# Sigmoid attention and a token-mixing MLP on one core: nine head groups exchange their halves by DMA instead of on GpSimd, with more buffers and a new order of work

## The chip, the core and the metric

The kernel runs on one core of a Trainium2 chip. The core has a matrix engine (TensorE, PE in the profile, its weight loads PEld), a vector engine (VectorE, DVE), an activation engine (ScalarE, ACT), GpSimd (POOL), and SyncE (SP), which here only issues DMAs. Each engine works through its own instructions in order and waits for the others by semaphores. SBUF is the on-chip memory of 128 partitions, PSUM the memory that TensorE writes. The metric is the device time of one execution in microseconds (us); the median of three runs of the kernel before is 209.17 us (208.95 to 209.36).

## The reference

Two stages, in float32, with batch B = 8, 12 heads, S = 448 tokens, 64 values per head, so D = 768:

```
scores = q @ k^T / 8 - log(448)            # per batch and head: 448 x 448
attn   = 1 / (1 + exp(-scores))            # sigmoid, no row sum
x      = attn @ v, the heads side by side  # (8, 448, 768)
wq, wk = x @ w_q, x @ w_k                  # 768 -> 64
mixed  = (wq @ wk^T / 8) @ x               # 448 x 448 token mixing, then 448 x 768
out    = max(mixed, 0) @ w_out             # 768 x 768
```

The kernel computes the mixing as wq @ (wk^T @ x), so the 448 x 448 matrix is never formed.

## The kernel before, in words

The 96 heads are handled as 24 groups n of four heads (three groups per batch). The tokens of a head are dealt to 64 positions of seven, so that a group's work falls into seven score steps, 168 in all. Work is done in these kinds of step, each with a letter in the string PLAN, and the loop at the end of the function emits the steps letter by letter. The string was written out by a planner beforehand; nothing is decided while the kernel runs.

- Loads and casts have no letter. ORDER lists them (q4, k4, v3 and so on; w0 to w6 are the weights). `pump_loads` issues a load on the SP queue as soon as, by program order, one of five load buffers (pool ld) is free; `pump` then emits the cast to bf16 on GpSimd (`cast1`, L184 and L194), provided that the cast buffers, two for q and k and three for v, are free by program order. On the chip the load waits for the cast that frees its buffer.
- q and k must be turned, so that the 64 values of a head lie on partitions. Kinds q/k and a/b do it with 56 or 14 TensorE transposes and one VectorE eviction (L242, L247). Kind c/d does it on VectorE: two stream transposes (L227) in 32 by 32 blocks of 4-byte pairs. Blocks do not cross a boundary of 32 partitions, so half of the data must first change places with its neighbour 32 partitions away. `arrange` does that on GpSimd with six copies, two each on L153, L156 and L159, of 32 partitions by 448 words. Of the 24 groups, 17 are of kind c, four of kind a (the first one included) and three of kind q.
- S is one score step: four 64 by 64 matmuls (L259) into a pair of PSUM banks and one sigmoid over 128 by 896 on ScalarE (L264). There are 168.
- P is one step of attn @ v (L277); seven of them fill a pair of banks, which VectorE evicts (L286, tile xt).
- x and X transpose xt (L317, L300) with an eviction (L330, L305); W, N, U and M are the projections, the transpose of wk, wk^T @ x, and the mixing with its relu; O is a piece of the product with w_out (L440, L475), and its last piece is evicted by VectorE (O) or ScalarE (o) and stored by DMAs on SP. Lower-case m, u and o are M, U and O with the eviction on ScalarE.
- C copies a weight tile to the other half of the partitions on VectorE (L664), six times two copies.

PSUM is handed out as four pairs of banks, so at most four of these steps can hold results that wait for their eviction. VectorE takes its instructions in the emitted order: a transpose that waits for GpSimd holds every eviction that stands behind it. `qk` tiles have eight buffers, `at` tiles 16, output tiles (`o`) three.

Of the kernel before, what the change touches and what calls it, by code (L numbers as in the profile page):

```python
# [9 lines left out]
F32 = mybir.dt.float32  # L10
BF16 = mybir.dt.bfloat16
# [6 lines left out]
def kernel(  # L18
# [43 lines left out]
    p_o = pool("o", 3)  # L62
    ps_q = pool("ps_q", 1, space=bass.MemoryType.PSUM)

# [47 lines left out]
    def xt(u, j):  # L112
# [10 lines left out]


    PLAN = (
        "SSSFFFKFSFSSSqkFPSPPPSPPPqSSSXSkSPPSPPPSSPaPSSPPPSbPPSxSSPPS"
        "SWSWWXScWSWdWPPPPSPPSPSNSUSaSbSabSSMSPCPSPMPPPSPPSPPSSWWPPSW"
        "PcdPSXSWWWSSqxkSMSPPSPPPPCSPcSoXSOSSdoSNOoSCOSPPPPSPPPCSPPPP"
        "SWWSXPSWCWSPPSUScWSSOdWOScOOSMdSPPPPMSPPSPcSONxSOSMSPPdPxSCP"
        "PPSPOSOSSWWOcWSPPPdSPPPPSOSWSSWOOWSUcSoSNOSPPPxdSPPSPcPSOOSS"  # L130
        "MPPPPSPdPPSoWSMSWOWSMWSXSPPcdPPSXSPPPSUScWSMooSdMSOWOSxOSOXS"
        "xOSOPSPPPSPPPPSPPPPScdPOSPOSOOSOOSMOSOSPPcPSdPPSPPooSONSOuSx"
        "SWWWXWWWSMOOSxoSOPcSPPPNdPSPPSoOmOOSoSoMSOOSUcSPcPSPPdPSPOPo"
        "SOSOSPPPPPPmPooSxSOdOSooSMoSoxWWWWWWSPMPPSPPcPSPOdSOONSOSoOS"
        "xoSOSooSUSoSOoSoPSoSOPPPPMPPPPPxPmPmPPWWWWoWWOxxNoouOOOMMmoO"
        "oOOOoOOoOoOoOooOoOo"
    )
    PLAN = "".join(PLAN)
    KIND = ["a"] + [t for t in PLAN if t in "qac"]

    ld = {}
    SRC = dict(q=q, k=k, v=v)
# [3 lines left out]
    def arrange(n, eng):  # L146

        arranged.add(n)
        w = pq[n].rearrange("p t e i d y -> p t e (i d y)").bitcast(U32)
        z = p_one.tile([P, 2, NI * 32], U32, tag="swap", name="swap")  # L150
        for g in range(2):
            lo, hi = slice(64 * g, 64 * g + 32), slice(64 * g + 32, 64 * g + 64)
            eng.tensor_copy(out=z[lo], in_=w[hi, :, 0])  # L153
        for g in range(2):
            lo, hi = slice(64 * g, 64 * g + 32), slice(64 * g + 32, 64 * g + 64)
            eng.tensor_copy(out=w[hi, :, 0], in_=w[lo, :, 1])  # L156
        for g in range(2):
            lo = slice(64 * g, 64 * g + 32)
            eng.tensor_copy(out=w[lo, :, 1], in_=z[lo])  # L159

    def load1(n, nm, eng):
        u, j = quads[n]
        if KIND[n] == "c" and nm != "v":
            t = p_ld.tile([P, 2 * NI * HD], F32, tag="ld", name=nm + "32")
            eng.dma_start(
                out=t, in_=SRC[nm][u, 4 * j : 4 * j + 4].rearrange("h (p r) d -> (h p) (r d)", r=2 * NI),
            )
# [3 lines left out]
        eng.dma_start(  # L171
            out=t,
            in_=SRC[nm][u, 4 * j : 4 * j + 4].rearrange(
                "(g h) (p i) d -> (h p) g (i d)", g=2, i=NI
            ),
        )
        ld[nm, n] = t

    def cast1(n, nm, eng):
        if KIND[n] == "c" and nm != "v":  # L180
# [3 lines left out]
            eng.tensor_copy(  # L184
                out=f[:, "qk".index(nm)].rearrange("p e i d y -> p e y i d"),
                in_=ld.pop((nm, n)).rearrange("p (y i e d) -> p e y i d", y=2, i=NI, e=2),
            )
# [6 lines left out]
        eng.tensor_copy(  # L194
            out=t16.rearrange("p i b d -> p b i d"),
            in_=ld.pop((nm, n)).rearrange("p b (i d) -> p b i d", i=NI),
        )
        ld[nm + "16", n] = t16
# [14 lines left out]
    def transposes_whole(ps, t16, r):  # L213

        for x, i in enumerate(range(r.start, r.stop)):
            nc.tensor.transpose(
                ps[:, x * P : (x + 1) * P], t16[:, i].rearrange("p b d -> p (b d)"), ident16,
            )

    def tr(n, nm, kind):  # L220
        t = "qk".index(nm)
        t16 = ld.pop((nm + "16", n))
        if kind in "cd":
            if t == 0:
                qk[n] = p_qk.tile([P, 2, 2, NI, NP], BF16, tag="qk", name="qk")
            assert n in arranged
            nc.vector.transpose(  # L227
                out=qk[n][:, t].rearrange("p h i n -> p (h i n)").bitcast(F32),
                in_=t16[:, t].rearrange("p e i d y -> p (e i d y)").bitcast(F32),
            )  # L230
            return
        if t == 0:
            ps_qk[n] = bank2()
        fb, _, ps = ps_qk[n]
        if kind in "ab":
            transposes_whole(ps[:, t], t16, slice(0, NI))
        else:
            transposes(ps[:, :, t * S : (t + 1) * S], t16, slice(0, NI))
        if t == 1:
            qk[n] = p_qk.tile([P, 2, 2, NI, NP], BF16, tag="qk", name="qk")  # L240
            if kind in "ab":
                nc.vector.tensor_copy(  # L242
                    out=qk[n].rearrange("p t h i n -> p t i h n"),
                    in_=ps[:, :, 0 : 2 * S].rearrange("p t (i h n) -> p t i h n", i=NI, h=2),
                )
            else:
                nc.vector.tensor_copy(  # L247
                    out=qk[n].rearrange("p t h i n -> p t h (i n)"),
                    in_=ps[:, :, 0 : 2 * S].rearrange("p h (t x) -> p t h x", t=2),
                )  # L250
            release(fb)
# [3 lines left out]
    def scores(n, i):  # L255
        fb, sc, _ = bank2()
        for g in range(2):
            for h in range(2):
                nc.tensor.matmul(  # L259
                    sc[HALF[h], g, 0:S], qk[n][HALF[g], 1, h, i, :],  # L260
                    qk[n][HALF[g], 0, h].rearrange("p i n -> p (i n)"), start=True, stop=True,
                )
        at = p_at.tile([P, 2, S], BF16, tag="at", name="at")
        nc.scalar.activation(at, sc[:, :, 0:S], ACTF.Sigmoid, bias=bias_t, scale=attn_scale)  # L264
        release(fb)
        ats[n, i] = at
# [286 lines left out]
    for t in wqks:  # L553
# [1 line left out]


    ORDER = (
# [5 lines left out]
    )  # L563
    ORDER = [(t[0], int(t[1:])) for t in ORDER.split()]
    used, loaded, cast = set(), set(), set()
# [15 lines left out]
    def pump():  # L581
        while len(cast) < len(ORDER) + 2:
# [11 lines left out]
                                in_=w32["qk"].rearrange("p (c n) -> p c n", c=NC)[HALF[h], g::2],  # L594
                            )
            else:
                back = 3 if nm == "v" else 2
                if n >= back and (nm, n - back) not in used:
                    break
                if nm != "v" and KIND[n] == "c" and n >= 2 and not {("q", n - 2), ("k", n - 2)} <= used:  # L600
                    break
                cast1(n, nm, nc.gpsimd)
            cast.add((nm, n))
# [13 lines left out]
    def tr_part(nm, t16, r, e):  # L617
        fb, _, ps = bank2()
        transposes_whole(ps[:, 0], t16, r)
        COPY[e](  # L620
            out=qk[0][:, "qk".index(nm), :, r].rearrange("p h i n -> p i h n"),
            in_=ps[:, 0, 0 : (r.stop - r.start) * P].rearrange("p (i h n) -> p i h n", h=2, n=NP),
        )
        release(fb)
# [4 lines left out]
    used |= {("q", 0), ("k", 0)}  # L629
    pump()  # L630

    done = dict.fromkeys("SPqkKxWNUMOC", 0)
    ALIKE = dict(a="q", c="q", b="k", d="k", X="x")
    done["q"] = done["k"] = 1

    for t in PLAN:
# [14 lines left out]
                pump()  # L651
        elif kind in "qk":
            tr(c, kind, t)
            used.add((kind, c))
            pump()
        elif t == "K":
            tr_part("k", k016, KB, "v")
        elif kind == "x":
# [55 lines left out]
```

## Time and profile before

| | |
|---|---|
| median of three runs | 209.17 us |
| the profiled execution: its own time / its span | 210.04 us / 208.2 us |
| granted TensorE clock, mean | 0.978 |
| busy, PE / ACT / POOL / DVE | 182.3 / 171.5 / 141.6 / 130.4 us |
| sigmoid L264: count, busy, mean | 168, 156.2 us, 1014 ns |
| stream transpose L227: count, mean | 34, 628 ns |
| GpSimd copies L153, L156, L159: count, mean | 3 x 34, 559 / 557 / 555 ns |
| HBM read / written | 35.78 / 11.01 MB |

The span is the profiled part of the execution; the execution's own time is 1.8 us longer. A busy TensorE is not TensorE at its peak, since matmuls overlap and their ends are modelled. "Idle before" is the time an engine stood still just before an instruction, with the engine and line that ended it. The sigmoids are the clock of the kernel: the first begins at 6.4 us and the last at 182.5 us, and where two follow each other directly their starts lie 0.906 us apart (the median).

### The profile page before, as it was taken

To read this page: it belongs to the slowest core of one execution; us is meant where nothing else is said; L and a number is where in the kernel's file an instruction comes from. 1 tells how busy PE (TensorE), PEld (TensorE's weight loads), DVE (VectorE), ACT (ScalarE), POOL (GpSimd) and SP (SyncE) were. 2 spreads that over 40 slices of the span, in tenths; PEclk is the share of its full clock that TensorE was granted. 3 is DMA by queue.
4 is the path that set the end of the run, shared out by engine and by line. 5 is a ranking of instruction groups with operands and counts; after the bars stand their busy time and mean duration, and the time that the engine had idled before them with its cause. 6 is when DMAs were issued, how large, how long until landed. Compare 5 with 4: busy or idle time off the path is not lost.

```text
span 208.2 us, 7853 instructions
## 1 busy us (share of the span) xinstructions
PE 182.3 (88%) x3324; PEld 110.0 (53%) x3324; DVE 130.4 (63%) x194; ACT 171.5 (82%) x197; POOL 141.6 (68%) x197
## 2 busy tenths in 40 slices
PE   7777888876889896899589699899999999999990
PEld 7343444533544352344345347676886868665560
DVE  3143455756769996955489575686867687374440
ACT  4898999986898998799779849988999989984510
POOL 2565997699899999999999999999398910000000
PEclk9999999999699999999999969999999999999997
DMA  6999988986978449876588687989475562461475
GB/s 176 362 353 265 303 284 268 348 266 217 318 242 290 155 118 324 258 278 197 180 249 289 234 251 217 296 290 340 163 214 163 172 154 51 110 154 34 137 213 151
DMA packets 24563, 47.30 MB, mean 227 GB/s; under 512 B 3792, under 2 KB 17744, under 8 KB 24528
## 3 DMA queue, kind: packets, MB, share of 16 engines
q1 hardware_dynamic: 23808, 45.42, 70.2%
q10 hardware_dynamic: 720, 1.38, 1.8%
q8 instruction: 26, 0.43, 0.8%
q14 instruction: 9, 0.07, 0.1%
HBM read 35.78 MB, written 11.01 MB: 225 GB/s over the span
## 4 chain that ended last, share of the span: by engine, by line
PE 43%; POOL 26%; DMA 11%; ACT 7%; issue 6%; DVE 4%; ACTq 1%; SPq 1%; POOLq 0%; DVEq 0%
PE banks L440 13%; PE banks L277 8%; PE banks L259 7%; PE banks L475 7%; POOL qk L184 6%; ACT at L264 6%; POOL qk L159 4%; POOL swap L153 4%; POOL qk L156 4%; DMA w<-in_moe_w_out_dram 3%; POOL v L194 3%; DMA w<-in_moe_w_k_dram 3%; PE banks L341 3%; DMA q<-in_q_dram 2%; DMA k<-in_k_dram 2%
## 5 line engine op out<-in xcount | busy, mean ns | idle before, releaser
L264 ACT ACTIVATE at<-banks,bias_t 128x896 bf16<-128x896 f32 x168 | 156.2, 1014 | 18.4 <-PE banks L259 15.8
L259 PE MATMUL banks<-qk 64*64 64x448 bf16 x672 | 63.5, 365 | 11.8 <-DVE mx L383 3.3
L277 PE MATMUL banks<-at,v 64*64 64x448 bf16 x672 | 45.6, 354 | 1.0 <-POOL v L194 0.7
L259 PEld LDWEIGHTS <-qk 64*64 64x64 bf16 x672 | 23.7, 106 | 35.5 <-issue 27.4
L440 PE MATMUL banks<-wout,mx 64*64 64x384 bf16 x672 | 35.4, 324 | 0.0
L475 PE MATMUL banks<-wout,mx 128*128 128x384 bf16 (+1 forms) x174 | 33.0, 328 | 0.1
L286 DVE CAST xt<-banks 128x896 bf16<-128x896 f32 x22 | 23.8, 1082 | 9.9 <-PE banks L277 9.7
L227 DVE STREAM_TRANSPOSE qk<-qk 128x448 f32<-128x448 f32 x34 | 20.7, 628 | 13.3 <-POOL qk L159 13.3
L277 PEld LDWEIGHTS <-v 64*64 64x64 bf16 x672 | 21.4, 107 | 12.6 <-POOL v L194 3.0
L440 PEld LDWEIGHTS <-mx 64*64 64x64 bf16 x672 | 22.9, 107 | 4.5
L383 DVE TENSOR_SCALAR mx<-banks 128x1024 bf16<-128x1024 f32 (+2 forms) x22 | 22.1, 1016 | 4.5 <-PE banks L395 3.9
L194 POOL CAST v<-v 128x896 bf16<-128x896 f32 x24 | 22.2, 932 | 3.4 <-DMA v<-in_v_dram 2.7
L184 POOL CAST qk<-k 128x896 bf16<-128x896 f32 x17 | 20.4, 1198 | 4.4 <-issue 3.1
L475 PEld LDWEIGHTS <-mx 128*128 128x128 bf16 x174 | 15.6, 99 | 13.6 <-issue 5.6
L184 POOL CAST qk<-q 128x896 bf16<-128x896 f32 x17 | 20.4, 1202 | 0.8 <-DMA q<-in_q_dram 0.6
L153 POOL COPY swap<-qk 32x448 uint32<-32x448 uint32 x34 | 19.0, 559 | 2.1
L156 POOL COPY qk<-qk 32x448 uint32<-32x448 uint32 x34 | 18.9, 557 | 2.0
L159 POOL COPY qk<-swap 32x448 uint32<-32x448 uint32 x34 | 18.9, 555 | 2.0
L341 PE MATMUL banks<-xt,wqk 128*128 128x448 bf16 x48 | 14.0, 360 | 3.3 <-DVE xt L286 2.6
L449 DVE COPY o<-banks 128x768 f32<-128x768 f32 x13 | 12.4, 955 | 6.9 <-PE banks L440 6.9
L505 DVE COPY o<-banks 128x384 f32<-128x384 f32 x20 | 11.1, 554 | 8.7 <-PE banks L475 8.3
L330 DVE COPY xn<-banks 128x1024 bf16<-128x1024 bf16 (+1 forms) x15 | 9.5, 636 | 4.5 <-PE banks L317 3.7
(68 smaller groups left out, 163.9 us busy)
## 6 DMA issues: line engine op xcount, KB each, us to landing
q<-in_q_dram SPq DMA_DIRECT2D x24, 448.0 KB, 5.0
v<-in_v_dram SPq DMA_DIRECT2D x24, 448.0 KB, 5.2
k<-in_k_dram SPq DMA_DIRECT2D x23, 448.0 KB, 5.7
out_dram<-o SPq DMA_DIRECT2D x48, 192.0 KB, 4.0
w<-in_moe_w_out_dram SPq DMA_DIRECT2D x6, 384.0 KB, 5.7
out_dram<-o ACTq DMA_DIRECT2D x6, 192.0 KB, 3.2
k<-in_k_dram SPq DMA_DIRECT2D x1, 256.0 KB, 4.5
k<-in_k_dram SPq DMA_DIRECT2D x1, 192.0 KB, 3.3
```

The costliest lines, as they stand in the source:

```text
L153: eng.tensor_copy(out=z[lo], in_=w[hi, :, 0])
L156: eng.tensor_copy(out=w[hi, :, 0], in_=w[lo, :, 1])
L159: eng.tensor_copy(out=w[lo, :, 1], in_=z[lo])
L184: eng.tensor_copy(out=f[:, "qk".index(nm)].rearrange("p e i d y -> p e y i d"), in_=ld.pop((nm, n)).rearrange("p (y i e d) -> p e y i d", ...
L194: eng.tensor_copy(out=t16.rearrange("p i b d -> p b i d"), in_=ld.pop((nm, n)).rearrange("p b (i d) -> p b i d", i=NI),)
L259: nc.tensor.matmul(sc[HALF[h], g, 0:S], qk[n][HALF[g], 1, h, i, :], qk[n][HALF[g], 0, h].rearrange("p i n -> p (i n)"), start=True, stop=True,
L264: nc.scalar.activation(at, sc[:, :, 0:S], ACTF.Sigmoid, bias=bias_t, scale=attn_scale)
L277: nc.tensor.matmul(ps[HALF[g], h, 0:S], ld["v16", n][HALF[h], i, g, :], ats[n, i][HALF[h], g, :], start=(i == 0), stop=(i == NI - 1),)
L286: nc.vector.tensor_copy(out=xt(u, j)[:, :, 0:S], in_=ps[:, :, 0:S])
L383: nc.vector.tensor_scalar(dst, ps, moe_scale, 0.0, ALU.mult, ALU.max)
L440: nc.tensor.matmul(ps[HALF[x], y, 0:NB], mx[HALF[y], u, b, 64 * (i - 3 * y) : 64 * (i - 3 * y) + 64], wout16[HALF[y], slot(y, b), x * NB : ...
L475: nc.tensor.matmul(ps, mxs[w][:, 2 * S * c + m * P : 2 * S * c + (m + 1) * P], wout16[:, c, w0:w1], start=(c == 0), stop=(c == NC - 1),)
```

## The change

Of the 24 groups seven are now of kind c (GpSimd exchanges the halves, as before), nine of a new kind e/f, six of kind q and two of kind a. A group of kind e/f is not arranged by GpSimd. VectorE transposes each of the two halves twice, once into `qk` and once into a new tile `mv` (two buffers): four stream transposes instead of two. A new step g then issues four DMAs on SP (`move`), each of 32 partitions by 1,792 bytes (56 KB), which put the quarters that belong 32 partitions away from `mv` into `qk`. The scores of that group wait for the four DMAs.

The load buffers go from five to eight, those of the cast v from three to four. The tile layouts of `qk` and of the cast pair change so that each half is contiguous. The two copies of a C step move 384 four-byte words instead of 768 bf16 values. PLAN and ORDER are new strings. In the new PLAN eight M steps instead of five carry the lower-case letter, and 45 O pieces instead of 41.

```diff
-    p_ld = pool("ld", 5)
+    p_ld = pool("ld", 8)
-    p_v16 = pool("v16", 3)
+    p_v16 = pool("v16", 4)
+    p_mv = pool("mv", 2)
...
     def arrange(n, eng):
         arranged.add(n)
-        w = pq[n].rearrange("p t e i d y -> p t e (i d y)").bitcast(U32)
+        if KIND[n] == "e":
+            return
+        w = pq[n].rearrange("p e t i d y -> p e (t i d y)").bitcast(U32)
...
+    moves = []
+
+    def move():
+        n, m = moves.pop(0)
+        for g in range(2):
+            for h in range(2):
+                own, other = 64 * g + 32 * h, 64 * g + 32 * (1 - h)
+                nc.sync.dma_start(
+                    out=qk[n][other : other + 32, h].rearrange("p t i n -> p (t i n)"), in_=m[own : own + 32, 1 - h],
+                )
+
     def tr(n, nm, kind):
         t = "qk".index(nm)
-        if kind in "cd":
+        if kind in "cdef":
+            assert n in arranged
+            w = pq[n].rearrange("p e t i d y -> p e (t i d y)").bitcast(F32)[:, t]
             if t == 0:
                 qk[n] = p_qk.tile([P, 2, 2, NI, NP], BF16, tag="qk", name="qk")
-            nc.vector.transpose(
-                out=qk[n][:, t].rearrange("p h i n -> p (h i n)").bitcast(F32),
-                in_=t16[:, t].rearrange("p e i d y -> p (e i d y)").bitcast(F32),
-            )
-            return
+            nc.vector.transpose(out=qk[n][:, t].rearrange("p t i n -> p (t i n)").bitcast(F32), in_=w)
+            if kind in "ef":
+                if t == 0:
+                    moves.append((n, p_mv.tile([P, 2, 2 * S], BF16, tag="mv", name="mv")))
+                nc.vector.transpose(out=moves[-1][1][:, t].bitcast(F32), in_=w)
+            return
...
-            if len(ring) >= 5 and ring[-5] not in cast:
+            if len(ring) >= 8 and ring[-8] not in cast:
...
-                back = 3 if nm == "v" else 2
+                back = 4 if nm == "v" else 2
...
+        elif t == "g":
+            move()
...
-                nc.vector.tensor_copy(out=wout16[HALF[y], NC + c, :], in_=wout16[HALF[1 - y], c, :])
+                nc.vector.tensor_copy(
+                    out=wout16[HALF[y], NC + c, :].bitcast(U32), in_=wout16[HALF[1 - y], c, :].bitcast(U32)
+                )
```

The kinds of the groups, in order, were and are:

```
before  a q q a c a a c q c c c c c c c c c c c c c c c
after   a q a q c q q c q q c e c e e e c e c e e e e c
```

Numbers of score steps (S letters) emitted between a group's g and its own first score step, for the nine e groups 11, 13, 14, 15, 17, 19, 20, 21, 22: 11, 7, 12, 15, 10, 7, 8, 8 and 3.

More of the change, by code (lines that the diff above doesn't have):

```diff
@@ L125 @@
     PLAN = (
[L126 to L136, printed above, removed]
+        "SSSFFKFSSFSqkFSPSFPSPPSPPPSaPSSbSPPSSPPPPXSPSqkSSPPPSXSSPPSP"
+        "WSXcSSdWSWWPWWPPSPNPSPSCPqSkSUCSPSXSPPPPMSPSPSqkSXMSSPPPPSPW"
+        "SPPcdSWWSMXSWWWSSCOqSOkSSPPPPNSPPPSUSCPCPSSPPPPqkSSPScWWoSOS"
+        "xWSoSdefWPPPSOSPPgPPSoSMSWOSWSOSMXSOSoMSOSPcSPPSPPPSePOdXSOf"
+        "SPPPSPPxSPPSOegSfNSgOOXSOSPCPPSPPPPSeWfWWgSOSSOWWWSPPPPSPPxS"
+        "PSUScoSdNOSMSePPPPPSPPSoWoMSxOOSMSWfoWSOScdPPPSgPPPPSUSWWWSx"
+        "SPPPPxSPPPSoSOMSoOSPPefSPPmOPPSPOSoOSOSOMSOOSePPPSgPPSoOSfPP"
+        "OSOSWWWNSSWXWWgUSxPPmePPPPSPoSOxSoSOSofONmOOSgoSOMSOOSuSOeSM"
+        "OOSOPScPPPPSPPSPPPfPSPPPSooSoMgSOWWWWWWmxONoSdxoSOSoOSxoSOSP"
+        "PPPSPSPPOOSOSOPPSPPPSPOoSPoSOSUPPSPOmPOPMmoPPoxWWWWWWOoxxNoo"
+        "uOommMOoOOooOooOoOooOoooOooo"
     )
     PLAN = "".join(PLAN)
-    KIND = ["a"] + [t for t in PLAN if t in "qac"]
+    KIND = ["a"] + [t for t in PLAN if t in "qace"]
     ld = {}
@@ L148, in arrange @@
         arranged.add(n)
-        w = pq[n].rearrange("p t e i d y -> p t e (i d y)").bitcast(U32)
-        z = p_one.tile([P, 2, NI * 32], U32, tag="swap", name="swap")
+        if KIND[n] == "e":
+            return
+        w = pq[n].rearrange("p e t i d y -> p e (t i d y)").bitcast(U32)
+        z = p_one.tile([P, 2 * NI * 32], U32, tag="swap", name="swap")
         for g in range(2):
             lo, hi = slice(64 * g, 64 * g + 32), slice(64 * g + 32, 64 * g + 64)
-            eng.tensor_copy(out=z[lo], in_=w[hi, :, 0])
+            eng.tensor_copy(out=z[lo], in_=w[hi, 0])
         for g in range(2):
             lo, hi = slice(64 * g, 64 * g + 32), slice(64 * g + 32, 64 * g + 64)
-            eng.tensor_copy(out=w[hi, :, 0], in_=w[lo, :, 1])
+            eng.tensor_copy(out=w[hi, 0], in_=w[lo, 1])
         for g in range(2):
             lo = slice(64 * g, 64 * g + 32)
-            eng.tensor_copy(out=w[lo, :, 1], in_=z[lo])
+            eng.tensor_copy(out=w[lo, 1], in_=z[lo])
     def load1(n, nm, eng):
         u, j = quads[n]
-        if KIND[n] == "c" and nm != "v":
+        if KIND[n] in "ce" and nm != "v":
             t = p_ld.tile([P, 2 * NI * HD], F32, tag="ld", name=nm + "32")
@@ L179, in cast1 @@
     def cast1(n, nm, eng):
-        if KIND[n] == "c" and nm != "v":
+        if KIND[n] in "ce" and nm != "v":
             if n not in pq:
@@ L184, in cast1 @@
             eng.tensor_copy(
-                out=f[:, "qk".index(nm)].rearrange("p e i d y -> p e y i d"),
+                out=f[:, :, "qk".index(nm)].rearrange("p e i d y -> p e y i d"),
                 in_=ld.pop((nm, n)).rearrange("p (y i e d) -> p e y i d", y=2, i=NI, e=2),
@@ L218, in transposes_whole @@
             )
+    moves = []
[7 more added lines that the diff above has]
+                )
     def tr(n, nm, kind):
         t = "qk".index(nm)
-        t16 = ld.pop((nm + "16", n))
-        if kind in "cd":
+        if kind in "cdef":
+            assert n in arranged
+            w = pq[n].rearrange("p e t i d y -> p e (t i d y)").bitcast(F32)[:, t]
             if t == 0:
                 qk[n] = p_qk.tile([P, 2, 2, NI, NP], BF16, tag="qk", name="qk")
-            assert n in arranged
-            nc.vector.transpose(
-                out=qk[n][:, t].rearrange("p h i n -> p (h i n)").bitcast(F32),
-                in_=t16[:, t].rearrange("p e i d y -> p (e i d y)").bitcast(F32),
-            )
+            nc.vector.transpose(out=qk[n][:, t].rearrange("p t i n -> p (t i n)").bitcast(F32), in_=w)
[3 more added lines that the diff above has]
+                nc.vector.transpose(out=moves[-1][1][:, t].bitcast(F32), in_=w)
             return
+        t16 = ld.pop((nm + "16", n))
         if t == 0:
@@ L242, in tr @@
                 nc.vector.tensor_copy(
-                    out=qk[n].rearrange("p t h i n -> p t i h n"),
+                    out=qk[n].rearrange("p h t i n -> p t i h n"),
                     in_=ps[:, :, 0 : 2 * S].rearrange("p t (i h n) -> p t i h n", i=NI, h=2),
@@ L247, in tr @@
                 nc.vector.tensor_copy(
-                    out=qk[n].rearrange("p t h i n -> p t h (i n)"),
+                    out=qk[n].rearrange("p h t i n -> p t h (i n)"),
                     in_=ps[:, :, 0 : 2 * S].rearrange("p h (t x) -> p t h x", t=2),
@@ L259, in scores @@
                 nc.tensor.matmul(
-                    sc[HALF[h], g, 0:S], qk[n][HALF[g], 1, h, i, :],
-                    qk[n][HALF[g], 0, h].rearrange("p i n -> p (i n)"), start=True, stop=True,
+                    sc[HALF[h], g, 0:S], qk[n][HALF[g], h, 1, i, :],
+                    qk[n][HALF[g], h, 0].rearrange("p i n -> p (i n)"), start=True, stop=True,
                 )
@@ L596, in pump @@
             else:
-                back = 3 if nm == "v" else 2
+                back = 4 if nm == "v" else 2
                 if n >= back and (nm, n - back) not in used:
                     break
-                if nm != "v" and KIND[n] == "c" and n >= 2 and not {("q", n - 2), ("k", n - 2)} <= used:
+                if nm != "v" and KIND[n] in "ce" and n >= 2 and not {("q", n - 2), ("k", n - 2)} <= used:
                     break
@@ L620, in tr_part @@
         COPY[e](
-            out=qk[0][:, "qk".index(nm), :, r].rearrange("p h i n -> p i h n"),
+            out=qk[0][:, :, "qk".index(nm), r].rearrange("p h i n -> p i h n"),
             in_=ps[:, 0, 0 : (r.stop - r.start) * P].rearrange("p (i h n) -> p i h n", h=2, n=NP),
@@ L630 @@
     pump()
-    done = dict.fromkeys("SPqkKxWNUMOC", 0)
-    ALIKE = dict(a="q", c="q", b="k", d="k", X="x")
+    done = dict.fromkeys("SPqkKxWNUMOCg", 0)
+    ALIKE = dict(a="q", c="q", e="q", b="k", d="k", f="k", X="x", g="g")
     done["q"] = done["k"] = 1
@@ L653 @@
             tr(c, kind, t)
-            used.add((kind, c))
-            pump()
+            if t in "df":
+                used.add(("q", c))
+            if t not in "ce":
+                used.add((kind, c))
+                pump()
+        elif t == "g":
+            move()
         elif t == "K":
```

10 rows, old and new, of the table ORDER are left out of this document.

## The prediction

> **What bounds the kernel now.** I read the page first (busy time, the row of slices, the chain), then cut the span where the sigmoids number 1, 21, 41 and so on begin, asked for the engines' busy time in those stretches, and last looked at the waits and at one stall.
>
> ```profile
> span 208.2 us, 7853 instructions
> PE 182.3 (88%) x3324; PEld 110.0 (53%) x3324; DVE 130.4 (63%) x194; ACT 171.5 (82%) x197; POOL 141.6 (68%) x197
> POOL 2565997699899999999999999999398910000000
> PE 43%; POOL 26%; DMA 11%; ACT 7%; issue 6%; DVE 4%; ACTq 1%; SPq 1%; POOLq 0%; DVEq 0%
> ...
> L227 DVE STREAM_TRANSPOSE qk<-qk 128x448 f32<-128x448 f32 x34 | 20.7, 628 | 13.3 <-POOL qk L159 13.3
> ```
>
> POOL is full from about 30 to 140 us and holds a quarter of the chain; the stream transposes waited 13.3 us for its last copy. The stretches (start:end, length, then busy PE, PEld, DVE, ACT, POOL):
>
> ```profile
> 25.20:44.20 19.00, 15.83 (x254) 8.55 (x257) 12.55 (x17) 18.19 (x21) 15.47 (x20) 1.00 0.89 293
> 44.20:66.00 21.80, 18.25 (x312) 9.69 (x305) 14.52 (x22) 18.56 (x20) 20.06 (x27) 0.92 0.80 268
> 66.00:87.30 21.30, 18.08 (x289) 8.29 (x282) 18.27 (x28) 18.74 (x22) 19.92 (x29) 1.00 0.70 219
> 87.30:108.40 21.10, 18.27 (x265) 9.00 (x264) 13.09 (x20) 18.49 (x21) 19.75 (x28) 1.00 0.71 226
> 108.40:131.60 23.20, 21.06 (x378) 12.19 (x372) 16.61 (x22) 18.97 (x23) 21.71 (x31) 0.93 0.81 246
> 131.60:154.30 22.70, 21.83 (x540) 17.19 (x534) 16.02 (x21) 20.34 (x24) 18.43 (x27) 1.00 0.81 266
> 154.30:176.00 21.70, 21.70 (x558) 16.30 (x554) 16.84 (x22) 20.51 (x24) 11.74 (x17) 1.00 0.49 140
> ```
>
> Each holds 20 sigmoids, 20 x 0.906 = 18.1 us. Steps 21 to 40 take 0.9 us more than that; steps 41 to 120, where POOL is 92 to 94% busy, 3.7, 3.2, 3.0 and 5.1 us more; after step 120 PE is full. How the lateness travels, from the timeline:
>
> ```profile
> 102.95 0.65 DVE L227 STREAM_TRANSPOSE qk<-qk 128x448 f32<-128x448 f32 x1 [2.42 <-POOL qk L159]
> 103.52 1.05 DVE L286 CAST xt<-banks 128x896 bf16<-128x896 f32 x1
> 104.62 0.38 PE L259 MATMUL banks<-qk 64*64 64x448 bf16 x4 [2.67 <-DVE xt L286]
> 105.10 1.01 ACT L264 ACTIVATE at<-banks,bias_t 128x896 bf16<-128x896 f32 x1 [1.95 <-DVE o L505]
> ```
>
> DVE waits for POOL, an eviction stands behind it, PE finds no free bank, the sigmoid starves. The sigmoid gaps that follow such a wait (steps 46, 77, 78, 97, 98, 111, 112: starts 2.77, 1.98, 1.88, 2.97, 1.51, 2.71 and 2.98 us apart) exceed 0.906 by 10.4 us in all. SP's own waits and two DMA prices:
>
> ```profile
> SPq L165 <- POOL v L194: 24.8, 12, 4.2
> SPq L171 <- POOL qk L184: 14.0, 10, 4.6
> SPq L458 <- DVE o L449: 12.3, 5, 4.5
> ...
> v<-in_v_dram SPq DMA_DIRECT2D x24, 448.0 KB, 5.2
> out_dram<-o SPq DMA_DIRECT2D x2, 48.0 KB, 2.2
> ```
>
> **The change, part by part.** To compare the two orders I priced every letter from its row and summed per 20 score steps of each PLAN. PE: 0.19 us a score, value or W step, 0.49 an output piece (twelve L440 matmuls in the chain), 0.4 to 0.7 a transpose or U; ACT 0.906 a sigmoid, its other rows as they stand; DVE 0.61 a stream transpose (20.7/34), other evictions by their means. Before to after:
>
> ```
> steps     measured  ACT          PE           DVE
> 1-40      37.8      36.2  36.2   23.8  24.3   19.5  21.1
> 41-60     21.8      18.1  18.1   14.5  14.2   16.6  13.4
> 61-120    65.6      54.8  55.8   48.6  49.5   48.5  54.9
> 121-168   50.9      46.7  47.0   49.7  49.0   36.5  38.6
> tail      25.7      10.0  12.2   22.2  22.1   11.9   8.1
> ```
>
> *POOL loses* ten arranges: 60 copies by 0.557 is 33.4 us, and casts come out 0.5 us cheaper (32 by 1.2 and 14 by 0.93 for 34 and 12), so 141.6 falls to about 108 us. Adding up its queue in order, with 0.61 us a copy, group 15's operands were ready 2.2 us, group 17's 2.0 us and group 19's 2.9 us before a clock of 0.93 us a score step, from 6.4 us on, wants them turned, which is no margin against one late bank; in the new order the least margin from group 10 on is 7.8 us and from group 12 on 11.9. So the waits for L159 go, and their 10.4 us of gaps are the gross gain. What is late next is DVE, and after step 120 PE.
>
> *DVE gains* 50 - 34 = 16 stream transposes, 9.8 us, and one more eviction of a kind q group, 1.1; C, M and O steps give some back. In steps 61 to 120 its sum becomes 54.9 us beside 55.8 of ACT: no room. There it was busy 48.5 of 65.6 us, waited 8.3 for POOL and stood idle 8.8 for other reasons. If all that other idle stays, the stretch takes 54.9 + 8.8 = 63.7 (-1.9); if half of it goes, 59.3 (-6.3). The floor is ACT's sum with the 0.9 us per 20 steps of steps 21 to 40, 55.8 + 2.7 = 58.5 (-7.1). I take the middle of the first two, 61.5: -4.1, since both are the same row read with and without what PE's lateness, itself due to POOL, put into that idle. The high end is no gain at all, if the e/f runs of four transposes (2.4 us against 1.2 for c/d) hold evictions as the late ones do now. Steps 41 to 60 have less DVE work and no POOL wait: 18.1 + 1.2 = 19.3, -2.5 (-0.5 to -2.8).
>
> *C copies* as words: the row is 12 copies, mean 687 ns, the fastest 355, the slowest 1250 where a GpSimd instruction ran beside them. No row has the new form; I take 0.4 each, near the fastest, within bounds of 0.18 and 0.69, that is 12 x 0.29 = 3.4 us less DVE work, already in the sums. [...]
>
> *The moves:* 36 DMAs on SP and 2.0 MB, beside 47.3. Issuing costs 0.33 to 0.45 us each (L165, L536), so 1.3 to 1.8 us a group, in which loads and stores behind them wait; eight load buffers cover that with POOL's margins (if not, a load that comes 2 us late costs nothing under 7.8). A move stands on SP behind loads that wait for POOL (mean 2.1 and 1.4 us, worst 4.6) and stores that wait for evictions. From g to landing: least 0 + 1.5 + 2.2 = 3.7 us, most 4.6 + 1.8 + 5.7 (a 448 KB k load) = 12.1, middle 7.7; the row nearest in size is the 2.2. The larger of the ACT and PE sums between g and the group's first score (DVE's for 13) leaves 10.0, 7.6, 10.9, 14.1, 10.1, 8.4, 10.1, 7.9 and 5.4 us. With 7.7 only group 22 would wait to speak of, 2.3 us; its moves stand behind stores and no load, so I take 1.0. Bounds 0 and 26 us (12.1 less each lead).
>
> *Loads and the rest:* steps 1 to 40 already run at ACT's pace; the new load order keeps POOL's first margins (4.4, 3.5, 2.6 us before; 3.5, 2.6, 2.6 after). Nothing, -0.8 to +1.5. Steps 121 to 168: PE's sum 49.0 and the 1.2 above it of before, and the 1.0: 51.2, +0.3. The tail has the same PE sum and the same chain from W over N and U to the last pieces: 0, within 1.
>
> Sum: 0 - 2.5 - 4.1 + 0.3 + 0 = -6.3. The profiled execution took 210.04 us (span 208.2 and 1.8 around it), 0.9 above the median of 209.17; a difference carries over, so the median is forecast at 202.9 us.
>
> **The rivals.** *DVE takes POOL's place:* steps 61 to 120 gain nothing, since the runs of transposes hold banks as POOL did, and only -2.5 + 0.3 remain: 207.0. For it speaks the DVE sum at 98% of ACT's; against it that transposes are emitted 6 to 18 steps ahead, and that nothing forces DVE to stand idle before them.
>
> *The moves come late (slower):* SP takes its queue in order, so a move behind a load that waits for POOL waits too, and PE, in order as well, stops at the group's first score. It costs the sum of what delivery exceeds the leads by: at 9.1 us 7.1, which cancels the gain of 6.3 (1.0 of it is counted already); at 10 us 10.7: 202.9 + 9.7 = 212.6. For it: SP waits that reach 4.6 us, and leads of 5.4 to 8.4 us for groups 13, 19, 21 and 22; against it: POOL is no longer behind, so the loads ahead of a move should wait less. [...]
>
> *More than half of DVE's other idle goes*, and the moves are free: -2.8 - 7.1 - 0.7 gives 198.6.
>
> **How the numbers follow.** A measurement of this kernel tells about 0.2%, 0.4 us, from no change. My forecast (201 to 206): 0.40. Larger gain (below 201): 0.10. DVE in POOL's place (206 to 208.75): 0.13. Within 0.2%: 0.04. Moves late: 0.25, and runs of transposes that cost more than POOL's waits did: 0.08, both above 209.6. Faster 0.63, same 0.04, slower 0.33. The range 200 to 213 leaves out half of the large gains and a good half of the late-move cases above 213; the forecast's own range is 201 to 206.
>
> **What would show it.** POOL busy near 108 us and no transpose waiting for its copies; 41 to 60 and 61 to 120 near 19.3 and 61.5 us; DVE busy about 89% of the latter; `qk<-mv` landing in 2 to 5 us; PE's weight loads at scores waiting for those DMAs about 1 us in all. Wrong if scores wait several microseconds for `qk<-mv`, if SP's moves stand behind loads, or if sigmoid gaps after runs of four transposes replace those after L159.

## The result and the profile after

The changed kernel takes 201.53 us (median of four, 200.84 to 202.29) beside 209.06 us for the kernel before: a ratio of 0.964, 95% interval 0.960 to 0.968. Run again beside the later experiments it took 0.960 (0.954 to 0.966) of the kernel before. The forecast was 202.9 us, range 200 to 213.

The page of the changed kernel, the lines that answer to those of before:

```profile
span 199.0 us, 8092 instructions
PE 180.0 (90%) x3440; PEld 110.4 (55%) x3440; DVE 135.4 (68%) x205; ACT 172.7 (87%) x202; POOL 107.0 (54%) x137
POOL 2577899999899396669797914051494100000000
PE 61%; ACT 15%; DVE 13%; issue 8%; ACTq 1%; DVEq 0%
...
L241 DVE STREAM_TRANSPOSE qk<-qk 128x448 f32<-128x448 f32 x32 | 19.5, 622 | 0.0
L245 DVE STREAM_TRANSPOSE mv<-qk 128x448 f32<-128x448 f32 x18 | 10.8, 602 | 0.0
qk<-mv SPq DMA_DIRECT2D x36, 56.0 KB, 3.5
```

GpSimd has left the chain (26% before) and is busy 107.0 us. The idle time before the stream transposes has gone from 13.3 us to 0.0: VectorE no longer waits for GpSimd. The moves land in 3.5 us (median). The stretches are cut again where sigmoids 1, 21, 41 and so on begin (start:end, length, then busy PE, PEld, DVE, ACT, POOL):

```profile
24.60:43.60 19.00, 15.75 (x316) 8.63 (x315) 14.96 (x20) 18.21 (x21) 18.09 (x26) 1.00 0.98 350
43.60:62.50 18.90, 16.82 (x323) 9.00 (x323) 14.78 (x22) 18.21 (x22) 17.93 (x23) 1.00 0.94 326
62.50:80.90 18.40, 18.13 (x241) 8.29 (x243) 15.21 (x24) 18.24 (x20) 11.66 (x16) 1.00 0.86 281
80.90:99.90 19.00, 17.85 (x310) 9.39 (x306) 18.04 (x30) 18.28 (x21) 15.01 (x18) 1.00 0.92 283
99.90:122.20 22.30, 20.51 (x432) 12.78 (x426) 18.22 (x26) 20.04 (x24) 15.87 (x19) 1.00 0.93 292
122.20:144.30 22.10, 21.14 (x522) 16.11 (x515) 16.76 (x25) 20.19 (x24) 5.87 (x7) 1.00 0.66 200
144.30:166.60 22.30, 21.87 (x550) 15.98 (x543) 17.05 (x22) 19.85 (x24) 7.59 (x11) 1.00 0.52 125
```

Up to step 100 the kernel now runs at ScalarE's pace: ScalarE is busy 18.2 us in stretches of 18.4 to 19.0. After that PE is nearly full, as it was: it is busy 20.5 to 21.9 us in stretches of 22.1 to 22.3. By stretch, from one profiled execution each:

```
steps     before  after  change  forecast
1-40       37.8   37.1    -0.7     0
41-60      21.8   18.9    -2.9    -2.5
61-120     65.6   59.7    -5.9    -4.1
121-168    50.9   51.2    +0.3    +0.3
tail       25.7   25.6    -0.1     0
```

These sum to -9.3 us, while the medians differ by 7.5: the profiled execution before lay 1.0 us above its median (210.04 beside 209.06) and the one after 0.7 us below (200.84 beside 201.53). The profile of the repeat gives 37.5, 18.3, 59.8, 52.2 and 25.7 us, so one profile tells a stretch to about 1 us.

One difference is not in the prediction: the granted TensorE clock (PEclk, the third column from the right in these rows) was 0.92 in steps 41 to 60 and 0.93 in steps 101 to 120 before, and is 1.00 in every stretch now. Before, it stood at 0.50 from 52.3 to 55.8 us and from 120.6 to 124.0 us, each time within 2 us of the end of a stop of PE (1.8 and 2.1 us long); a stop of 2.7 us that ended at 104.6 us has no such stretch behind it. So part of what the waits for GpSimd cost may have been paid as slower matmuls behind them (those of L475 started 320 ns apart at 0.50, from 120.6 us on, and 162 ns apart at 1.00, medians of the kernel before); no run here separates that part.

### The profile page after: what moved, and what is told of

The parts are those of the page before. It is cut to its first block, busy times and chain, and to the rows that moved or that the text cites. A ratio compares the mean times of both kernels' runs of the same rounds, so it can differ in the third digit from the quotient of the medians.

```text
span 199.0 us, 8092 instructions
## 1 busy us (share of the span) xinstructions
PE 180.0 (90%) x3440; PEld 110.4 (55%) x3440; DVE 135.4 (68%) x205; ACT 172.7 (87%) x202; POOL 107.0 (54%) x137
## 3 DMA queue, kind: packets, MB, share of 16 engines
q10 hardware_dynamic: 720, 1.38, 1.9%
## 4 chain that ended last, share of the span: by engine, by line
PE 61%; ACT 15%; DVE 13%; issue 8%; ACTq 1%; DVEq 0%
ACT at L280 14%; PE banks L456 14%; PE banks L275 12%; PE banks L293 11%; PE banks L491 10%; DVE wout L685 4%; PE banks L357 4%; PE banks L388 3%; DVE xt L302 2%; PE banks L566 2%; PE banks L333 1%; PE banks L411 1%; DVE mx L399 1%; PE banks L423 1%; DVE qk L263 1%
## 5 line engine op out<-in xcount | busy, mean ns | idle before, releaser
L280 ACT ACTIVATE at<-banks,bias_t 128x896 bf16<-128x896 f32 x168 | 154.2, 1016 | 7.6 <-PE banks L275 6.9
L275 PEld LDWEIGHTS <-qk 64*64 64x64 bf16 x672 | 25.8, 105 | 30.7 <-issue 22.9
L302 DVE CAST xt<-banks 128x896 bf16<-128x896 f32 x23 | 24.9, 1085 | 13.7 <-PE banks L293 11.9
L187 POOL CAST qk<-k 128x896 bf16<-128x896 f32 x16 | 19.1, 1200 | 21.0 <-DVE mv L245 14.7
L293 PEld LDWEIGHTS <-v 64*64 64x64 bf16 x672 | 22.7, 106 | 9.7 <-issue 2.5
L399 DVE TENSOR_SCALAR mx<-banks 128x1024 bf16<-128x1024 f32 (+2 forms) x20 | 19.7, 999 | 9.5 <-PE banks L423 6.2
L197 POOL CAST v<-v 128x896 bf16<-128x896 f32 x24 | 22.1, 936 | 4.5 <-PE banks L293 3.7
L187 POOL CAST qk<-q 128x896 bf16<-128x896 f32 x16 | 19.1, 1204 | 6.1 <-issue 4.4
L491 PEld LDWEIGHTS <-mx 128*128 128x128 bf16 x174 | 15.0, 97 | 13.3 <-issue 5.6
L521 DVE COPY o<-banks 128x384 f32<-128x384 f32 x16 | 8.7, 544 | 5.0 <-PE banks L491 4.4
L521 ACT COPY o<-banks 128x384 f32<-128x384 f32 x11 | 5.3, 479 | 6.5 <-PE banks L491 6.5
L245 DVE STREAM_TRANSPOSE mv<-qk 128x448 f32<-128x448 f32 x18 | 10.8, 602 | 0.0
L397 ACT ACTIVATE mx<-banks 128x448 bf16<-128x448 f32 (+1 forms) x10 | 7.0, 738 | 2.8 <-PE banks L411 2.4
```

What stands on the lines that cost most here:

```text
L187: eng.tensor_copy(out=f[:, :, "qk".index(nm)].rearrange("p e i d y -> p e y i d"), in_=ld.pop((nm, n)).rearrange("p (y i e d) -> p e y i d ...
L197: eng.tensor_copy(out=t16.rearrange("p i b d -> p b i d"), in_=ld.pop((nm, n)).rearrange("p b (i d) -> p b i d", i=NI),)
L275: nc.tensor.matmul(sc[HALF[h], g, 0:S], qk[n][HALF[g], h, 1, i, :], qk[n][HALF[g], h, 0].rearrange("p i n -> p (i n)"), start=True, stop=True,
L293: nc.tensor.matmul(ps[HALF[g], h, 0:S], ld["v16", n][HALF[h], i, g, :], ats[n, i][HALF[h], g, :], start=(i == 0), stop=(i == NI - 1),)
L302: nc.vector.tensor_copy(out=xt(u, j)[:, :, 0:S], in_=ps[:, :, 0:S])
L399: nc.vector.tensor_scalar(dst, ps, moe_scale, 0.0, ALU.mult, ALU.max)
```

## The experiments

All ratios are to the kernel before on the same chip. The theory: the gain is GpSimd's relief, and VectorE and the moves' delivery are what limits it next. The main rival: the new order and the deeper buffers bring the gain, whoever exchanges the halves.

**Each half of the change alone.** First the new order and buffers without the relief: all nine e/f groups back to c/d.

```diff
-    PLAN = <the string>
+    PLAN = <the string>.replace("e", "c").replace("f", "d").replace("g", "")
```

> The changed kernel with its order of work, eight load buffers and word copies, but all nine e/f groups back to c/d: GpSimd exchanges the halves of 16 groups again, no moves, two stream transposes a group. Theory (the gain is GpSimd's relief): GpSimd's work goes back from 107 to about 140 us, its copies again arrive last from about step 80 on, and the time goes back to 206 to 212 us, with waits for the last arrange copy of 8 us or more. Rival (the new order and the buffers bring the gain, whoever exchanges the halves): 200.5 to 202.5 us.

Measured: 210.02 us, ratio 1.011 (1.005 to 1.016), so 1.1% slower than before although everything but the moves and their transposes is in. The row of steps 61 to 120 and the waits for GpSimd in it:

```profile
62.00:132.10 70.10, 60.07 (x966) 31.41 (x968) 46.00 (x66) 57.43 (x63) 63.54 (x90) 0.95 0.72 236
```

```profile
DVE qk L241 <- POOL qk L159: 9.5, 7, 2.9
PEld L293 <- POOL v L197: 5.4, 1, 5.4
```

The 60 steps take 70.1 us instead of 59.7, VectorE waits 9.5 us for GpSimd's copies, and once TensorE waits 5.4 us for a cast of v that stands behind them. The loss sits mostly in one place: the sigmoids of steps 101 and 102 start 7.4 us apart, and the granted clock is 0.50 from 105.9 to 112.5 us. Outside this stretch it is no slower than the changed kernel (36.9, 18.3 and 50.6 us). The rival falls: without the relief the new order is worth less than nothing.

Then the relief without the new order: the kernel before, with the nine groups turned by four stream transposes and four moves each, issued right behind the last transpose.

```diff
-    "...cd..."                # nine of the 17 c/d groups of the old string
+    "...efg..."
```

> The kernel before with its own order, five load buffers, three value buffers and bf16 copies; only the nine groups 11, 13, 14, 15, 17, 19, 20, 21 and 22 are turned with four stream transposes and the four moves, issued right behind the last transpose. Theory: GpSimd's waits go (8.3 us of them lie in steps 61 to 120), but the old order leaves only 3 to 8 score steps between the transposes and the first score, so some scores wait for the moves: 203 to 208 us. Rival (without the new order nothing is gained): 208.5 to 210. Rival (moves late decides): above 210, with several microseconds of score waits for the moved data.

Measured: 248.02 us (243.8 to 249.0; the profile is of the longest). Who waited, in us, times and longest; the last line is from SP's own waits:

```profile
POOL qk L187 <- DVE mv L245: 54.8, 5, 15.0
PEld L275 <- DMA qk<-mv: 33.5, 11, 8.6
PE banks L275 <- DMA qk<-mv: 31.6, 11, 8.3
...
SPq L168 <- POOL qk L187: 28.8, 16, 11.2
```

This is the rival of late moves. Its 40 us cannot be set against the 9.7 us that the prediction priced, since that went by the leads of the new order. Seven of the nine groups begin with a gap of 3.3 to 9.6 us between sigmoid starts; in the changed kernel no score waited for a move (0.2 us in its repeat). The waits form a ring: GpSimd's casts wait for the transposes into `mv` to free the cast buffers (54.8 us), loads on SP wait for those casts (28.8 us), the moves stand in SP's queue behind the loads (in seven groups the first move is issued 2.9 to 6.3 us after the last transpose ends), the scores wait for the moves, and PE's lateness holds VectorE's evictions and the next transposes. The granted clock falls with it, to 0.919 in the mean. The old order with moves and eight load buffers was not tried. So neither half gains anything alone, as far as these two runs go.

**How near the moves are to being late.** Each move takes a second hop through another tile.

```diff
+        m2 = p_mv.tile([P, 2, 2 * S], BF16, tag="mv2", name="hop")
...
-                nc.sync.dma_start(out=qk[n][other : other + 32, h], in_=m[own : own + 32, 1 - h])
+                nc.sync.dma_start(out=m2[other : other + 32, h], in_=m[own : own + 32, 1 - h])
+        for g in range(2):
+            for h in range(2):
+                other = 64 * g + 32 * (1 - h)
+                nc.sync.dma_start(out=qk[n][other : other + 32, h], in_=m2[other : other + 32, h])
```

> The changed kernel, but each move goes through a second tile: four DMAs from mv into it, then four from it into qk, which SP issues when the first four have landed. This adds one landing (2.0 to 6.8 us, median 3.5, in the changed kernel) and four issues of 0.6 us, about 6 us, to each delivery, and holds SP as long. In the changed kernel the first sigmoid of an e/f group begins 4.1 to 7.4 us after the last move was issued, that is 0 to 3 us after the matmul could start by the median landing. Theory (delivery has little in hand): scores wait for the moves in most groups, 206 to 225 us. Rival (the leads are ample and the moves far off the path): below 203 us.

Measured: 226.08 us, ratio 1.078 (1.072 to 1.083), just above the expected span.

```profile
PEld L280 <- DMA qk<-hop: 21.0, 22, 3.4
PE banks L280 <- DMA qk<-hop: 14.0, 18, 3.0
```

From the first issue to the last landing a group now takes 9.5 us in the middle (6.9 to 10.3), where the changed kernel took 5.3 (4.4 to 7.9): 4.2 us more, not 6. That costs 24.6 us (226.1 less 201.5), of which PE stood still 14.0 us for the moved data; the granted clock is 0.961. The changed order has just enough lead, not plenty: by its trace the last of the four moves landed 0.3 to 0.8 us before the weight load that needs it in five of the nine groups (13, 14, 15, 17, 21), and 1.7 to 4.1 us before it in the others. Much of the lead goes into SP's queue: the first move of a group was issued 0.1 to 10.5 us (median 3.9) after its transposes had ended, for groups 13 to 15 right behind a load.

**What the moves cost where they are.** The same kernel without the step g; the scores of the nine groups are then computed from halves that were not exchanged.

```diff
-    PLAN = <the string>
+    PLAN = <the string>.replace("g", "")
```

> The changed kernel without its 36 moves: the nine e/f groups compute their scores from halves that were not exchanged, everything else as it is. Theory: the moves are hidden, no score waited for them, so 200.5 to 202.0 us (the 1.0 us that the sum gave them is at most this). Rival (the moves cost through SP's queue and the DMA rings, holding loads and stores): 197 to 200 us.

Measured: 199.37 us, ratio 0.952 (0.948 to 0.956), against 0.964 and 0.960 of the two measurements of the changed kernel: the moves cost 0.8 to 1.2% of 209 us, 1.7 to 2.5 us. That lies in the rival's span, so the theory that the moves are free falls, though the profile does not show the rival's mechanism, loads or stores held by the moves. What shows is a stop of PE in the middle of an output piece, for nothing that the profile names, after step 124. The changed kernel, its repeat, and the kernel without the second transposes (below), one line each from their timelines:

```profile
126.02 0.97 PE L456 MATMUL banks<-wout,mx 64*64 64x384 bf16 x17 [0.96 <-issue]
```

```profile
126.95 0.97 PE L456 MATMUL banks<-wout,mx 64*64 64x384 bf16 x17 [1.78 <-issue]
```

```profile
125.59 0.97 PE L457 MATMUL banks<-wout,mx 64*64 64x384 bf16 x17 [2.33 <-issue]
```

In these three it stops before the same 17 matmuls of 24; without the moves there is no stop at this place. Another such stop, after step 119, is 1.79 and 1.86 us in the changed kernel and its repeat and 1.23 us without the moves. Together that is 1.5 and 2.4 us, about what the moves cost. But the stops do not follow the moves alone. The two are 1.7 and 0.1 us with all moves and five load buffers, 1.2 us and none with all nine groups given back to GpSimd, 2.5 us and none with three groups by moves, and 1.2 and 1.0 us with five (these runs are below and above). So what the moves' price consists of stays open.

**VectorE's price.** Eighteen stream transposes more, and eighteen fewer. In the second, the moves copy a tile of zeros and the exchanged quarters are wrong.

```diff
                 nc.vector.transpose(out=moves[-1][1][:, t].bitcast(F32), in_=w)
+                extra = p_mv.tile([P, 2 * S], BF16, tag="extra", name="extra")
+                nc.vector.transpose(out=extra.bitcast(F32), in_=w)
```

> The changed kernel with a third stream transpose into a spare tile after each pair in the e/f groups: 18 more, 11.0 us of VectorE work, about two thirds of it before step 120, where VectorE is 86% busy (51.5 of 59.7 us in steps 61 to 120). Theory (VectorE is nearly the bound there): 204 to 208 us, the loss in steps 61 to 120. Rival (VectorE's idle time takes it): 201 to 202.5 us.

```diff
-                    moves.append((n, p_mv.tile([P, 2, 2 * S], BF16, tag="mv", name="mv")))
-                nc.vector.transpose(out=moves[-1][1][:, t].bitcast(F32), in_=w)
+                    moves.append((n, mv0))      # set to zero once
```

> The changed kernel without the 18 stream transposes into mv; the moves copy a tile of zeros instead, so the exchanged quarters are wrong; 10.8 us less VectorE work. Theory (VectorE is nearly the bound in steps 61 to 120): 199 to 200.5 us. Rival (VectorE's second transposes are hidden): 201 to 202 us.

Measured: 205.61 us, ratio 0.980 (0.976 to 0.984), and 199.03 us, ratio 0.949 (0.944 to 0.953). Against 0.964 or 0.960 the added 11 us of work cost 1.6 to 2.0% (3.3 to 4.1 us), the removed 10.8 us save 1.1 to 1.5% (2.4 to 3.2 us). Both fall on the side of the theory. Steps 61 to 120 with more, and with fewer:

```profile
62.20:125.20 63.00, 57.17 (x970) 30.66 (x972) 57.50 (x90) 57.08 (x63) 42.03 (x50) 1.00 0.85 274
```

```profile
62.20:120.40 58.20, 56.44 (x967) 30.35 (x969) 45.67 (x66) 56.56 (x64) 43.08 (x51) 1.00 0.91 293
```

VectorE's work there is 57.5, 51.5 (as changed) and 45.7 us and the stretch takes 63.0, 59.7 and 58.2: the first 6 us cost 1.5, the next 6 cost 3.3. About a third of VectorE's added time is on the path, and the share is rising. (In the kernel with fewer, steps 121 to 168 take 52.6 us, with the 2.33 us stop shown above in them.)

**The buffers.** The kernel before with eight load buffers and four for values:

```diff
-    p_ld = pool("ld", 5)
+    p_ld = pool("ld", 8)
...
-    p_v16 = pool("v16", 3)
+    p_v16 = pool("v16", 4)
```

> The kernel before with eight load buffers and four value buffers, nothing else. Theory: GpSimd is what is late, not the loads, so 208.5 to 209.5 us and GpSimd as full as before between 44 and 132 us. Rival (deeper loading is worth time by itself): 204 to 207 us.

Measured: 207.00 us, ratio 0.993 (0.990 to 0.997). That misses the theory's span and lies at the edge of the rival's. GpSimd is as full as before (59.8 of 63.9 us in steps 61 to 120), yet steps 1 to 40 fall from 37.8 to 36.3 us, steps 41 to 60 from 21.8 to 18.1 and steps 61 to 120 from 65.6 to 63.9, while steps 121 to 168 rise from 50.9 to 55.6:

```profile
43.10:61.20 18.10, 16.97 (x312) 8.97 (x304) 14.33 (x22) 18.05 (x20) 17.36 (x22) 1.00 0.90 303
61.20:125.10 63.90, 55.87 (x920) 29.08 (x916) 47.68 (x69) 56.13 (x62) 59.80 (x85) 1.00 0.73 236
125.10:180.70 55.60, 51.80 (x1236) 38.87 (x1232) 35.28 (x45) 47.48 (x53) 31.49 (x45) 0.97 0.54 158
```

In the kernel before, GpSimd had stood still for loads of w_out just ahead of this; with eight buffers it does not:

```profile
36.55 0.83 POOL L588 CAST wout<-w 128x768 bf16<-128x768 f32 x1 [1.44 <-DMA w<-in_moe_w_out_dram]
...
40.21 0.83 POOL L588 CAST wout<-w 128x768 bf16<-128x768 f32 x1 [0.95 <-DMA w<-in_moe_w_out_dram]
```

The loss of the deeper loading, in its own timeline:

```profile
132.15 0.57 SPq L165 DMA_DIRECT2D k<-in_k_dram  x1
...
133.85 0.96 DVE L449 COPY o<-banks 128x768 f32<-128x768 f32 x1 [4.17 <-DMA out_dram<-o]
133.94 2.78 SPq L458 DMA_DIRECT2D out_dram<-o  x4
134.87 0.38 PE L259 MATMUL banks<-qk 64*64 64x448 bf16 x4 [3.80 <-DVE o L449]
```

VectorE needs an output buffer whose store has not left, and PE stands behind it: the new wait is one for an output store. On SP the stores share the queue with loads that wait for GpSimd (L165 here). So by these profiles deeper loading is worth 6.8 us up to step 120, 3.6 of them in steps 41 to 60, and gives 4.7 us back later.

And the changed kernel with five load buffers:

```diff
-    p_ld = pool("ld", 8)
+    p_ld = pool("ld", 5)
...
-            if len(ring) >= 8 and ring[-8] not in cast:
+            if len(ring) >= 5 and ring[-5] not in cast:
```

> The changed kernel with five load buffers instead of eight, nothing else. The kernel before with eight buffers gained 3.6 us in steps 41 to 60 and lost most of it later. Theory (steps 41 to 60 are won by the deeper loads, not by less VectorE work or GpSimd's relief): those 20 steps go from 18.9 back to 20.5 to 22 us, GpSimd waits for loads of w_out again, and the time is 203 to 206 us. Rival (the new order alone gives that stretch): 201 to 202 us and 18.9 us there.

Measured: 205.96 us, ratio 0.989 (0.982 to 0.996), beside 200.65 for the changed kernel run with it. Steps 1 to 40 take 41.7 us instead of 37.5 and steps 41 to 60 20.7 instead of 18.3; steps 61 to 120 are equal (59.8), and steps 121 to 168 are shorter (50.3 beside 52.2). GpSimd waits for w_out, and PE for what GpSimd does next:

```profile
41.09 0.83 POOL L604 CAST wout<-w 128x768 bf16<-128x768 f32 x1 [1.17 <-DMA w<-in_moe_w_out_dram]
41.98 0.56 POOL L366 COPY wq<-wqk 64x448 bf16<-64x448 bf16 x1
...
42.59 0.58 PE L423 MATMUL banks<-wq,tmp 64*64 64x448 bf16 x2 [2.96 <-POOL wq L366]
```

So the theory of this run holds, and steps 1 to 40, of which it said nothing, lose most.

**The weight copies.** The changed kernel with C in bf16 again:

```diff
-                    out=wout16[HALF[y], NC + c, :].bitcast(U32), in_=wout16[HALF[1 - y], c, :].bitcast(U32)
+                    out=wout16[HALF[y], NC + c, :], in_=wout16[HALF[1 - y], c, :]
```

> The changed kernel with the weight copies between partition halves in bf16 again (768 values instead of 384 words). The changed kernel's word copies took 739 ns in the mean beside 687 of the bf16 ones before, from 357 to 1252. Theory: their length is set by the GpSimd instruction beside them, not by their form, so 201.0 to 202.0 us and again a mean of 0.65 to 0.8 us. Rival (the form halves them when GpSimd leaves them alone): the mean goes to about 1 us or more and the time to 202.5 to 204.

Measured: 200.58 us, ratio 0.966 (0.962 to 0.970): the same, with a mean of 761 ns a copy. In words they take no less than the 687 ns of before:

```profile
L685 DVE COPY wout<-wout 64x384 uint32<-64x384 uint32 x12 | 8.9, 739 | 0.3
```

**Fewer moves.** The changed kernel once more, with groups 19 to 22 given back to GpSimd, and with 15 and 17 as well (their e, f become c, d and their g goes).

> The changed kernel itself once more, on the chip of the runs beside it, so that differences of 1 us can be told: 0.960 to 0.968 of the kernel before, about 201.5 us.

> The changed kernel with groups 19 to 22 back to c/d, so that five groups are exchanged by moves and eleven by GpSimd, which stands idle most of the time after step 120. Without the moves the kernel took 0.952 and without the second transposes 0.949 of the kernel before, against 0.964: about 2.5 and 3.2 us for nine groups, 0.6 us each. Theory (the moves and second transposes of late groups buy nothing, since GpSimd has the time): 199.0 to 200.8 us. Rival (GpSimd's copies of late groups come last again, as with all groups back): above 202 us.

> The same with groups 15 and 17 back as well: three groups by moves (11, 13, 14), thirteen by GpSimd. With all nine back, the gaps came at steps 81 to 120. Theory (the relief is needed just there): worse than the version with five moved groups, 200 to 204 us, with waits for the last arrange copy. Rival (fewer moves are better throughout): below the version with five, 198 to 200 us.

Measured: 200.65 us, ratio 0.960 (0.954 to 0.966); 201.03 us, 0.965 (0.958 to 0.972); 207.43 us, 0.993 (0.989 to 0.998). Giving back the four late groups changes nothing that these runs can tell, so the saving of 0.6 us a group that was expected of it did not come; giving back 15 and 17 too loses nearly all of the gain. It was expected to be worse than the version with five, but not by so much. A gap of 5.8 us between sigmoids follows step 101, as with all nine given back (7.4); in the changed kernel there is none. TensorE waits 3.6 us there for a cast of v, and VectorE waits 2.8 us in all for copies of GpSimd (L159). A gap after step 119 (4.7 us) tells nothing of GpSimd: every kernel with the new order has it, the changed one 3.6 us, and the stop described above is part of it. The relief pays when it includes groups 15 and 17, and no version with all results right is clearly faster than the changed kernel.

## Why the prediction was right, point by point

- *POOL's waits go, 10.4 us of gaps gross.* Right. GpSimd was put near 108 us and takes 107.0, no stream transpose waits for its copies, and with its copies back steps 61 to 120 are 10.4 us longer (70.1 beside 59.7). That this equals the 10.4 us of gaps is chance: most of it is one gap in another order, with the clock at half in it and behind it.
- *Steps 61 to 120, -4.1 by VectorE's sum of 54.9 plus 6.6 of idle.* The direction was right and the size came out near by two errors that partly cancel; it is -5.9. VectorE was busy 51.5 us and idle 8.2. The sum was 3.4 too large, and the other idle, 8.8 before, was put at 6.6 and hardly shrank. (That 8.8 rested on the priced sum of 48.5; the rows show VectorE busy 48.0 us there, which makes it 9.3.) Part of the 3.4 is the price of a stream transpose: in a run of four they start 0.52 to 0.56 us apart (117.38, 117.94, 118.47, 118.99 us in the timeline), and the 31 in this stretch kept VectorE busy 17.5 us, 1.4 less than 0.61 each. What bounds the stretch is nearer to the floor that the prediction gave, ScalarE's pace of 58.5 us: it takes 59.7, and still 58.2 with 6 us less of VectorE's work.
- *Steps 41 to 60, -2.5 through less VectorE work and no wait for POOL.* The size was right (-2.9) by luck, the cause was not: eight load buffers alone give it to the kernel before, five take it from the changed one, and the new order with all nine groups back at GpSimd has it too (18.3 us). GpSimd was late there because loads, of w_out above all, were. The prediction had put the loads at nothing.
- *C copies, 0.4 us each.* Wrong: 0.74, no less than in bf16, and without effect on the time. No run shows the 0.4 or its lower bound of 0.18: words took 739 ns in the mean, bf16 values 687 before and 761 in the changed order. The spread from 357 to 1252 ns goes with the GpSimd instruction beside them: by the trace of the changed kernel 11 of the 12 copies end 0.21 us after such an instruction ends, and the other one took 357 ns; of the bf16 copies before it is 10 of 12, and the other two took 355 and 356 ns. No run here changes GpSimd's part alone.
- *The moves, 1.0 us of score waits.* Wrong in place, mis-sized by a little: no score waited, yet the moves cost 1.7 to 2.5 us. An issue took 0.59 us (median; 0.52 to 1.18), not 0.33 to 0.45, and the moves did stand behind loads, one of the prediction's signs of being wrong; the leads covered it.
- *Steps 121 to 168 and the tail.* As forecast, +0.3 and about 0, the first in part by luck: its 1.0 us of score waits did not come, PE's stops did, and the repeat gives +1.3.
- *The rival of late moves.* Not the case, but its break-even was real: with 4.2 us more delivery the kernel is slower than before by 17 us, and in the old order by 40. Its price was the plain sum of what delivery exceeds the leads by (10.7 us at 10 us delivery). In the second-hop run PE stood 14.0 us for moves and the loss was 24.6; the rest is, by the author's estimate, lateness that travels on, which that sum leaves out: GpSimd waited 22.1 us for the transposes into `mv` (16.1 in the changed kernel) and VectorE 16.0 for PE's value steps before its casts into `xt` (11.9), and the granted clock was 0.961 (1.00).
- *The rival of VectorE in POOL's place.* In between: about a third of VectorE's added time is on the path.

## What to carry to other kernels

Where a profile shows one engine late and a second engine's in-order queue standing behind it, take work from the late engine, but move the start of the replacement as far ahead of its consumer as its whole delivery takes: here the moves were part of a gain of 3.6% in an order that gave them leads of 5 to 14 us by the prediction's sums, and in the old order, with three to eight score steps, the kernel took a fifth longer. Price a replacement by what it adds to the next engine's sum per stretch, and add up whole queues with their due points; that forecast each stretch within 2 us, though in one of them for the wrong reason. Look at the granted clock beside the waits: it differed between these two kernels (0.978 and 1.00 in the mean), and the prediction had left it out. Separate what deeper loading gives from what the relief gives, by trying each alone.

## What the runs showed of the hardware that was not expected

PE stopped in the changed kernel with no wait that the profile names, longest 1.79 us before 119.55 us and 0.96 us before 126.02 us, each time in the middle of one step. In the trace's DMA records a 16 KB transfer of the queue q8, whose kind the page gives as instruction, began at 117.17 and took 0.93 us, and one began at 123.56 and took 0.99: both stops end 1.45 and 1.47 us after such a transfer ended. In the repeat the same two places stop 1.86 and 1.78 us, 1.41 and 1.36 us after the end of the transfers that began at 117.33 and 124.61. Two shorter stops in the changed kernel, 0.45 and 0.43 us, end 1.36 and 1.38 us after such a transfer, and the kernel before has one of 0.87 us, ending at 135.59 us, 1.29 us after one. Most of the 27 transfers of 16 KB are followed by no stop. That PE stood still because of these transfers is the author's estimate from these times; no run was made that changes them alone, and with five load buffers the second stop is 0.1 us although the moves are there. Another surprise is the store that held an eviction for 4.17 us when the loads on its queue were made deeper.
